# Global queries' pieces of an attention step: from its middle, into a half of the score bank, to its end, into the output bank of the step before

## The chip, the cores and the metric

One core of a Trainium2 chip runs the whole program in one launch. The metric is device time in microseconds; lower is better. TensorE does matrix products and transposes, VectorE (DVE in the rows) and ScalarE (ACT) read PSUM and work element by element, GpSimd (POOL) does some element work in SBUF, SyncE (SP) issues the transfers.

## The reference, cut to what matters

```python
# attention (batch 4, 8 heads, 512 local and 32 global tokens, head size 64, window 32)
s_g = scale * np.matmul(q_g, k_all.transpose(0, 1, 3, 2))
out_g = np.matmul(sm(s_g), v_all)
s_ll = np.where(mask, s_ll, -1000000000.0)      # mask: |i - j| <= 32
s_l = np.concatenate([s_lg, s_ll], axis=-1)
out_l = np.matmul(sm(s_l), np.concatenate([v_g, v_l], axis=2))
# dense layer on 2176 tokens, 512 -> 2048 -> 512
h = x @ w_in
g = np.maximum(h, 0.0) + alpha * np.minimum(h, 0.0)
x = g @ w_out
# 8 experts, 272 tokens each
h = np.maximum(x[mask] @ w1[e], 0.0)
out[mask] = h @ w2[e]
```

## The kernel before, in words

The program has three parts: attention, a dense layer over all tokens, and the experts. The change touches attention alone, the first 148 us.

Attention goes over 16 units (a batch and two heads); two units make a pair `p`, and a pair is done in four **steps** `j` = 0 to 3 of 128 local queries each, so there are 32 steps `n = 4p + j`, and three more in which the pipeline runs empty. The order on TensorE, VectorE and ScalarE is that in which `attention()` calls its helpers (`manual_schedule`); each engine takes its instructions strictly in that order. One turn of the loop holds work of four steps of the pipeline:

- `scores(n)`: TensorE writes the scores into two PSUM banks `s[0]` and `s[1]`, one for each head, 256 of 512 columns each (L387). VectorE makes four masked reductions of them (L393, out `pr` and the row maxima `mx`), ScalarE four exponentials (L395), GpSimd adds a small number to the sums (L397).
- `ptrans(n-1)`: four transposes of the probabilities (L403), copied to SBUF by ScalarE (L405, `pt`).
- `pv(n-2)`: probabilities by values into the lower 256 columns of an output bank `o` (L415); `norm` divides on VectorE (L421, L423).
- `oturn(n-3)`: the normalised output is transposed back into the upper 256 columns of its own `o` bank (L430), and copied into `xb` (L432), by VectorE in odd turns and by ScalarE in even ones.

There are two `o` banks, so the bank that `oturn` reads in turn `n` is the one that `pv` writes in turn `n+1`. Before turn 12 TensorE also makes two products of no use into `o` (L545) in most turns; from turn 12 on `dense.products` puts six products of the dense layer there (L613), with a negative part on ScalarE (L576, `neg`), the activation on VectorE (L591, `g`) and a rounding on ScalarE (L72, `ghi`). `fill` puts in the decoding of weights from float64: L83 and L72 on ScalarE, L85, L88, L90, L92 on VectorE, two or four of them in a turn.

The **global queries** of a pair are done in four pieces, one in a turn, by `wide_part`: in `j` = 1 `gscores` (L449; two reductions L456 on VectorE, then one long exponential L460 on ScalarE), in `j` = 3 `gtrans` (six transposes L472, copies L473 on both engines), in `j` = 0 of the next pair `gpv` (L482, scaled by VectorE, L485), in `j` = 2 `gturn` (L492, copied by VectorE, L493). Before the change they stand after the dense products and ahead of `pv`, and write into the unused upper half of `s[1]` of the same turn (`gscores` and `gtrans` also into a bank of their own, `gs` and `gt`).

Of the kernel before, what the change touches and what calls it, by code (L numbers as in the profile page):

```python
# [25 lines left out]
def tile_attention_moe_moe(ctx: ExitStack, tc: tile.TileContext, qkw, vw,  # L26
# [285 lines left out]
    with ExitStack() as at:  # L312
# [57 lines left out]
        def scores(p, j):  # L370
# [9 lines left out]
            s = d["s"] = [bank([128, 512], "s") for _ in range(2)]  # L380
            for pr in range(2):
                for h, r in heads():
                    for w in range(2):
                        i = 4 * j + 2 * pr + w
                        for a in range(2):
                            u = 2 * p + a
                            T.matmul(s[h][lane(w, a), pr * KW:pr * KW + KW], queries(u, i)[r], U[u]["k"][r, kpos(i):kpos(i) + KW],  # L387
                                     start=True, stop=True)
            for ii in range(4):
                pr, h = divmod(ii, 2)  # L390
                m = mask[:, 0 if j == pr == 0 else 2 if j == STEPS - 1 and pr else 1]
                sc = d["pr", j][:, ii]
                V.tensor_tensor_reduce(out=sc, in0=s[h][:, pr * KW:pr * KW + KW], in1=m, scale=-D ** -0.5, scalar=BIG,  # L393
# [46 lines left out]
        def gscores(p, part):  # L440
            d = G[p]
            if part == 0:
                d["mx"] = gp.tile([128, 4], F32, name="gmx", bufs=2)
            mx = d["mx"]
            s = d["s"][1][:, 256:256 + SG] if part else bank([128, S], "gs0")
            for a in range(2):
                k = U[2 * p + a]["k"]
                x = k[:, WIN:2 * WIN] if part else k[:, GO:GE + WIN].rearrange("p (m c) -> p m c", c=3 * WIN)[:, :, :2 * WIN]
                T.matmul(s[64 * a:64 * a + 64], U[2 * p + a]["g"], x, start=True, stop=True)  # L449
            if part:  # L450
                to, x, z = gsc[:, 2 * WIN:3 * WIN], s, gzero.to_broadcast([128, SG])
            else:
                to = gsc[:, :GE + WIN - GO].rearrange("p (m c) -> p m c", c=3 * WIN)[:, :, :2 * WIN]
                x = s.rearrange("p (m c) -> p m c", c=2 * WIN)
                z = gzero.unsqueeze(2).to_broadcast([128, S // (2 * WIN), 2 * WIN])
            V.tensor_tensor_reduce(out=to, in0=x, in1=z, scale=-D ** -0.5, scalar=mx[:, 0:1] if part else BIG,  # L456
                                   op0=OP.add, op1=OP.min, accum_out=mx[:, part:part + 1])
            if part:
# [3 lines left out]
                later.append(lambda: V.reciprocal(mx[:, 3:4], mx[:, 2:3]))  # L462

        def gtrans(p, part):
            d = G[p]
            n = 2 if part else 4
            t = d["s"][1][:, 256:].rearrange("p (n q) -> p n q", q=128) if part else bank([128, n, 128], "gt0")
            if not part:
                d["t"] = gp.tile([128, len(GW), 128], F32, name="gt")
            for i in range(n):  # L470
                o = kpos(GW[4 * part + i]) - GO
                T.transpose(t[:, i], d["p"][:, o:o + KW], ident)  # L472
            soon.append(lambda: (V.tensor_copy if part else A.copy)(d["t"][:, 4 * part:4 * part + n], t))  # L473

        def gpv(p, s):
            d = G[p]
            o = s[:, 256:256 + D]
# [7 lines left out]
            soon.append(lambda: V.tensor_scalar(d["o"], o, d["mx"][:, 3:4], None, op0=OP.mult))  # L485

        def gturn(p, s):
# [1059 lines left out]
```

## Time and profile before

| | us |
|---|---|
| median of 3 runs | 806.9 (805.6 to 809.14) |
| the profiled execution, its own time | 810.19 |
| its span, first to last instruction | 808.4 |
| TensorE busy | 767.9 (95%) |
| VectorE busy | 439.8 (54%) |
| ScalarE busy | 390.2 (48%) |

In the rows, "PE" is TensorE's products and "PEld" its weight loads; a bracket at the end of a row says how long the engine stood idle before it and what ended that. Ends of matmuls are modelled, so starts are what to read there. Rows of the same instruction that follow each other on VectorE and ScalarE start somewhat before the one ahead has ended, so what an instruction takes of its engine is read from start to start.

### The profile page before, as it was taken

The page shows a single profiled execution, that of the slowest core. Times are in us where ns is not written, and L with a number is a line of the kernel's source. Part 1 is how long each engine was busy: PE and PEld are TensorE (multiplying, and loading weights), DVE is VectorE, ACT ScalarE, POOL GpSimd, SP SyncE. Part 2 cuts the span into 40 slices and gives each one's busy share as a digit, 9 for nine tenths or more (in the row PEclk, how much of TensorE's full clock was granted, in tenths as well). Part 3 has the DMA queues.
Part 4 walks back from the last instruction along what each step waited for, and adds up shares of the span by engine and source line. Part 5 has one row for each costly group of instructions (what it writes and reads, how often), then busy time and mean ns, then how long its engine had stood idle before and what let it go on. Part 6 is the DMA issues. An engine that isn't in the chain of part 4 may idle for free.

```text
span 808.4 us, 21039 instructions
## 1 busy us (share of the span) xinstructions
PE 767.9 (95%) x8386; PEld 710.8 (88%) x8386; DVE 439.8 (54%) x1555; ACT 390.2 (48%) x967; POOL 367.7 (45%) x348
## 2 busy tenths in 40 slices
PE   6788889998999999999999999999899999999996
PEld 4556667998999989999999999999899999989994
DVE  4778887365445621433433467777667777651210
ACT  5768788344544543333332425342455554454430
POOL 2233333144443552100000738573699988688611
PEclk9999999999999999999999999999999999999999
DMA  9978893532343102012211236243376757557510
GB/s 342 385 267 318 287 345 129 202 106 86 118 134 103 63 30 83 29 56 81 88 58 55 84 100 221 92 142 98 106 208 212 207 190 206 155 175 212 192 46 28
DMA packets 53851, 121.98 MB, mean 151 GB/s; under 512 B 4600, under 2 KB 26040, under 8 KB 51705
## 3 DMA queue, kind: packets, MB, share of 16 engines
q1 hardware_dynamic: 50825, 111.73, 42.4%
q0 software_dynamic: 2928, 8.92, 3.1%
q8 instruction: 65, 1.06, 0.5%
q14 instruction: 33, 0.27, 0.1%
HBM read 102.80 MB, written 17.83 MB: 149 GB/s over the span
## 4 chain that ended last, share of the span: by engine, by line
PE 75%; DVE 7%; DMA 5%; issue 5%; ACT 4%; POOL 3%; SPq 0%; POOLq 0%; ACTq 0%; DVEq 0%
PE h L200 21%; PE h L1303 10%; PE h L1147 10%; PE y L239 9%; PE h L1167 8%; DMA raw<-in_moe_w_dram 2%; PE o L415 2%; DMA raw<-in_moe_w_in_dram 2%; PE h L1380 2%; PE t L403 2%; PE lp L282 2%; POOL m L73 2%; PE s L387 2%; DVE pr L393 1%; DMA xpart<-xd 1%
## 5 line engine op out<-in xcount | busy, mean ns | idle before, releaser
L73 POOL TENSOR_TENSOR m<-raw,m 128x1024 fp32r<-128x1024 f32 x64 | 152.2, 2398 | 16.8 <-ACT m L72 15.1
L200 PE MATMUL h<-xh,win 128*128 128x272 f32 x704 | 139.7, 293 | 2.3 <-ACT xd L245 2.3
L200 PEld LDWEIGHTS h<-xh,win 128*128 128x128 f32 x704 | 113.0, 190 | 4.6 <-ACT xd L245 2.5
L73 POOL TENSOR_TENSOR gr<-gb,gr 128x272 fp32r<-128x272 f32 x64 | 48.0, 773 | 148.9 <-ACT gr L72 148.5
L1147 PE MATMUL h<-xsh,m 128*128 128x272 f32 x512 | 103.3, 294 | 0.0
L200 PE MATMUL h<-xl,win 128*128 128x272 f32 x352 | 102.0, 290 | 0.0
L1303 PE MATMUL h<-gr,wout 128*128 128x272 f32 x672 | 95.1, 294 | 0.0
L1167 PE MATMUL h<-hh,m 128*128 128x272 f32 x448 | 91.4, 295 | 0.0
L1303 PEld LDWEIGHTS h<-gr,wout 128*128 128x128 f32 x672 | 87.0, 189 | 0.4 <-ACT gr L72 0.4
L239 PE MATMUL y<-ghi,wout 128*128 128x272 f32 x448 | 86.9, 290 | 0.0
L73 POOL TENSOR_TENSOR glo<-g,ghi 128x272 fp32r<-128x272 f32 x64 | 55.1, 868 | 69.3 <-ACT ghi L72 51.8
L72 ACT CAST m<-raw 128x1024 fp32r<-128x1024 f32 x64 | 66.0, 1050 | 40.1 <-DMA raw<-in_moe_w_dram 39.7
L1147 PEld LDWEIGHTS h<-xsh,m 128*128 128x128 f32 x512 | 81.7, 188 | 0.1
L205 ACT ACTIVATE neg<-h 128x272 f32<-128x272 f32 x120 | 47.6, 397 | 70.3 <-PE h L200 69.0
L1147 PE MATMUL h<-xsl,m 128*128 128x272 f32 x256 | 74.0, 292 | 0.0
L206 DVE SCALAR_TENSOR_TENSOR g<-neg,al,h 128x272 f32<-128x272 f32 x56 | 27.4, 496 | 84.4 <-ACT neg L205 71.5
L1167 PEld LDWEIGHTS h<-hh,m 128*128 128x128 f32 x448 | 71.4, 188 | 0.9 <-issue 0.9
L239 PEld LDWEIGHTS y<-ghi,wout 128*128 128x128 f32 x448 | 70.9, 188 | 0.8 <-issue 0.8
L200 PEld LDWEIGHTS h<-xl,win 128*128 128x128 f32 x352 | 67.1, 191 | 0.0
L1167 PE MATMUL h<-hl,m 128*128 128x272 f32 x224 | 65.8, 294 | 0.0
L239 PE MATMUL y<-glo,wout 128*128 128x272 f32 x224 | 64.5, 288 | 1.1 <-POOL glo L73 1.1
L206 DVE SCALAR_TENSOR_TENSOR gb<-neg,al,h 128x272 f32<-128x272 f32 x64 | 31.3, 496 | 58.8 <-ACT neg L205 58.8
(294 smaller groups left out, 1601.8 us busy)
## 6 DMA issues: line engine op xcount, KB each, us to landing
raw<-in_moe_w_dram SPq DMA_DIRECT2D x64, 512.0 KB, 4.4
vv<-in_v_dram SPq DMA_DIRECT2D x16, 1024.0 KB
qk<-in_qk_dram SPq DMA_DIRECT2D x14, 720.0 KB, 10.1
raw<-in_moe_w_in_dram SPq DMA_DIRECT2D x16, 512.0 KB, 3.9
raw<-in_moe_w_out_dram SPq DMA_DIRECT2D x16, 512.0 KB, 3.6
xb<-xs SPq DMA_DIRECT2D x15, 544.0 KB, 4.0
xs<-xb SPq DMA_DIRECT2D x16, 272.0 KB, 6.4
xpart<-xd SPq DMA_DIRECT2D x32, 136.0 KB, 3.1
```

The costliest lines, as they stand in the source:

```text
L72: a = A.copy(hi, src)
L73: return a, (lo_eng or V).tensor_tensor(lo, src, hi.bitcast(F32), op=OP.subtract)
L200: T.matmul(ps, wi[:, w, k, fs], x[:, k], start=i == 0, stop=i == 3 * KD - 1)
L205: A.activation(out=neg, in_=ps, func=AF.Relu, scale=-1.0)
L206: epi[0] = V.scalar_tensor_tensor(g, neg, al1[:, hf * KH + f:hf * KH + f + 1], ps, op0=OP.mult, op1=OP.add)
L239: T.matmul(ps, wo[:, w, f, ds_], x[:, f], start=f == 0 and i == 0, stop=f == KH - 1 and i == 2)
L282: T.matmul(lp[r:r + 32], w, x, start=n < 4, stop=n >= LT - 4)
L387: T.matmul(s[h][lane(w, a), pr * KW:pr * KW + KW], queries(u, i)[r], U[u]["k"][r, kpos(i):kpos(i) + KW], start=True, stop=True)
L403: T.transpose(t[:, ii], d["pr", j][:, ii], ident)
L1147: T.matmul(ps, d["w1"][:, w, kk, f * 128:(f + 1) * 128], x[:, kk], start=kk == 0 and i == 0, stop=kk == KD - 1 and i == 2)
L1167: T.matmul(ps, d["w2"][:, w, f, ms], x[:, f], start=i == 0, stop=i == 3 * K3 - 1)
L1303: T.matmul(ps[j], wo[:, w, f, ds_], x, start=f == 0 and a == 0, stop=f == KH - 1 and a == 2)
```

## The change: what it does, and the diff

`wide_part` is called after `oturn`, at the end of a turn, and its instructions write into `prev`, the `o` bank of the turn before, columns 0 on, whose lower half `norm` has read by then. The copy into `xb` is taken out of `oturn` into `oput` and stands behind the pieces. The readers of the pieces on VectorE and ScalarE move with them: behind `norm` and behind the copy `pt`. The score banks hold 256 columns only. `gscores` goes unit by unit, and its reciprocal moves to `gtrans`.

```diff
-            s = d["s"] = [bank([128, 512], "s") for _ in range(2)]
+            s = [bank([128, 2, KW], "s") for _ in range(2)]
...
+        def oput(p, j):
+            d = G[p]
+            o = d["o", j]
             x = d["x"][:, :, SG + QS * j:SG + QS * j + QS].rearrange("p a (w q) -> p w a q", q=WIN)
             at_out[0] = (A.copy if j % 2 else V.tensor_copy)(x, o[:, 256:].rearrange("p (w a q) -> p w a q", a=2, q=WIN))
 
...
-        def gscores(p, part):
...
+        def gscores(p, free):
             d = G[p]
-            if part == 0:
-                d["mx"] = gp.tile([128, 4], F32, name="gmx", bufs=2)
-            mx = d["mx"]
-            s = d["s"][1][:, 256:256 + SG] if part else bank([128, S], "gs0")
+            d["mx"] = mx = gp.tile([128, 4], F32, name="gmx", bufs=2)
+            s = (bank([128, S], "gs0"), free[:, :SG])
             for a in range(2):
...
+            def rest_():
+                V.tensor_tensor_reduce(out=gsc[:, :GE + WIN - GO].rearrange("p (m c) -> p m c", c=3 * WIN)[:, :, :2 * WIN],
+                                       in0=s[0].rearrange("p (m c) -> p m c", c=2 * WIN),
+                                       in1=gzero.unsqueeze(2).to_broadcast([128, S // (2 * WIN), 2 * WIN]),
+                                       scale=-D ** -0.5, scalar=BIG, op0=OP.add, op1=OP.min, accum_out=mx[:, 0:1])
+                V.tensor_tensor_reduce(out=gsc[:, 2 * WIN:3 * WIN], in0=s[1], in1=gzero.to_broadcast([128, SG]), scale=-D ** -0.5,
+                                       scalar=mx[:, 0:1], op0=OP.add, op1=OP.min, accum_out=mx[:, 1:2])
                 d["p"] = gp.tile([128, GE - GO], F32, name="gpr")
                 A.activation(out=d["p"], in_=gsc[:, :GE - GO], func=AF.Exp, bias=mx[:, 1:2], scale=-1.0, accum_out=mx[:, 2:3])
                 P.tensor_scalar(mx[:, 2:3], mx[:, 2:3], 1e-9, None, op0=OP.add)
-                later.append(lambda: V.reciprocal(mx[:, 3:4], mx[:, 2:3]))
...
+        def gtrans(p, free):
             d = G[p]
-            n = 2 if part else 4
-            t = d["s"][1][:, 256:].rearrange("p (n q) -> p n q", q=128) if part else bank([128, n, 128], "gt0")
-            if not part:
-                d["t"] = gp.tile([128, len(GW), 128], F32, name="gt")
-            for i in range(n):
-                o = kpos(GW[4 * part + i]) - GO
-                T.transpose(t[:, i], d["p"][:, o:o + KW], ident)
-            soon.append(lambda: (V.tensor_copy if part else A.copy)(d["t"][:, 4 * part:4 * part + n], t))
-
-        def gpv(p, s):
...
-        later, soon, at_out = [], [], [None]
-
-        def wide_part(n):
+        at_out = [None]
+
+        def wide_part(n, free):
             p, j = divmod(n, STEPS)
-            last = n - STEPS * NU // 2
-            if last >= 0:
-                s = bank([128, 512], "s") if last in (0, 1) else None
-            else:
-                s = G[p]["s"][1]
-            if j == 1 and last < 0:
-                gscores(p, 0)
-                gscores(p, 1)
+            last = n >= STEPS * NU // 2
+            if j == 0 and p:
+                gpv(p - 1, free)
+            if j == 1 and not last:
+                gscores(p, free)
+            if p and (j == 2 or last and j == 1):
+                gturn(p - 1, free)
             if j == 3:
-                gtrans(p, 0)
-                gtrans(p, 1)
-            if p and j == 0:
-                gpv(p - 1, s)
-            if p and (j == 2 or last == 1):
-                gturn(p - 1, s)
+                gtrans(p, free)
 
...
                 dense.products(n)
-                if n < N + 2:
-                    wide_part(n)
-                while soon:
-                    soon.pop(0)()
                 fill("V", 2 if n >= SOLO and n % 3 == 0 else 1 if n < SOLO else 0)
...
                     ptrans(*divmod(n - 1, STEPS))
                 if n >= 3:
                     oturn(*divmod(n - 3, STEPS))
+                if n < N + 2:
+                    wide_part(n, bank([128, 512], "o") if n == 1 else prev)
+                if n >= 3:
+                    oput(*divmod(n - 3, STEPS))
+                prev = o
                 if p and j == 3:
                     gout(p - 1)
```

What this does to the order. In turn 13 (`j` = 1) on TensorE stood, before (`s` the score banks, `gs` a bank of its own, `o` the output bank, `t` transposed probabilities):

```order
L449 MATMUL gs_1200<-qk 64x512 x2
L449 MATMUL s<-qk 64x32 [waits DVE_49]
L449 MATMUL s<-qk 64x32
L415 MATMUL o<-vv,pt 32x64 [waits Activation_49]
L415 MATMUL o<-vv,pt 32x64 x15
L403 MATMUL t<-ident,pr 128x128 x4
L430 MATMUL o<-ident,on 128x128 x2
L387 MATMUL s<-qk 32x128 [waits PE_49]
```

and there stands now, in the same turn, with the head of the next turn's scores and the `pv` of that turn behind it:

```order
L414 MATMUL o<-vv,pt 32x64 [waits Activation_49]
L414 MATMUL o<-vv,pt 32x64 x15
L402 MATMUL t<-ident,pr 128x128 x4
L429 MATMUL o<-ident,on 128x128 x2
L450 MATMUL gs_1229<-qk 64x512
L450 MATMUL o<-qk 64x32
L450 MATMUL gs_1229<-qk 64x512
L450 MATMUL o<-qk 64x32
L387 MATMUL s<-qk 32x128 [waits DVE_49,PE_49]
...
L414 MATMUL o<-vv,pt 32x64 [waits DVE_49,DMAHW0_49,PE_49,Activation_49]
```

The global pieces have gone behind the transposes and lost their wait for VectorE; the wait for VectorE stands at the next turn's `pv`.

On ScalarE, from the end of turn 13 over turn 14 (`j` = 2), stood before:

```order
L460 ACTIVATE gpr,gmx<-gsc,gmx 128x736 [waits DVE_49]
L405 COPY pt<-t 128x512 [waits PE_49]
L576 ACTIVATE neg<-h_1087 128x272
L395 ACTIVATE pr,sm<-pr,mx 128x128 [waits DVE_49,Activation_49]
L395 ACTIVATE pr,sm<-pr,mx 128x128 [waits DVE_49] x3
L72 CAST ghi<-g 128x272 [waits DVE_49]
L405 COPY pt<-t 128x512 [waits PE_49,Activation_49]
L432 COPY xb<-o 128x4x2x32 [waits PE_49]
```

and there stands now:

```order
L404 COPY pt<-t 128x512 [waits PE_49]
L460 ACTIVATE gpr,gmx<-gsc,gmx 128x736 [waits DVE_49]
L568 ACTIVATE neg<-h_1088 128x272
L394 ACTIVATE pr,sm<-pr,mx 128x128 [waits DVE_49,Activation_49]
L394 ACTIVATE pr,sm<-pr,mx 128x128 [waits DVE_49] x3
L72 CAST ghi<-g 128x272 [waits DVE_49]
L404 COPY pt<-t 128x512 [waits PE_49,Activation_49]
L435 COPY xb<-o 128x4x2x32 [waits DVE_49]
```

The long exponential of the global queries has changed places with the copy `pt`, and the copy into `xb` waits for VectorE where it waited for TensorE.

On VectorE, in turn 13, stood before:

```order
L456 ISA gsc,gmx<-gs_1200,gzero 128x8x64 [waits PE_49]
L456 ISA gmx 128x1
L456 ISA gsc,gmx<-s,gzero,gmx 128x32 [waits DVE_49,PE_49]
L456 ISA gmx 128x1
L421 RECIPROCAL sm<-sm 128x4
L423 TENSOR_TENSOR on<-o,sm 128x256 [waits DVE_49,PE_49]
L432 COPY xb<-o 128x4x2x32 [waits PE_49]
```

and there stands now:

```order
L420 RECIPROCAL sm<-sm 128x4
L422 TENSOR_TENSOR on<-o,sm 128x256 [waits DVE_49,PE_49]
L453 ISA gsc,gmx<-gs_1229,gzero 128x8x64 [waits PE_49]
L453 ISA gmx 128x1
L457 ISA gsc,gmx<-o,gzero,gmx 128x32 [waits DVE_49,PE_49]
L457 ISA gmx 128x1
L435 COPY xb<-o 128x4x2x32
```

The reductions of the global scores have gone behind the normalisation, and the copy into `xb` stands behind them.

## Rows read from the trace of the kernel before

**Rows 1.** Busy time by stretch: length, PE, PEld, DVE, ACT, POOL, granted clock, DMA share, GB/s.
```profile
200.00:260.00 60.00, 60.00 (x480) 59.01 (x479) 30.74 (x50) 29.13 (x64) 25.84 (x25) 1.00 0.39 120
```

**Rows 2.** The same view of a stretch of attention.
```profile
100.00:120.00 20.00, 17.85 (x429) 13.52 (x424) 17.97 (x79) 17.62 (x60) 7.50 (x11) 1.00 0.90 326
```

**Rows 3.** Waits, 0 to 150 us: who, for whom; total us, times, longest.
```profile
PE s L482 <- ACT pr L395: 3.1, 3, 1.6
...
PE s L492 <- DVE mx L393: 1.9, 5, 0.9
...
PE s L482 <- DVE mx L393: 1.6, 4, 0.6
...
PE s L472 <- DVE mx L393: 1.0, 2, 0.7
```

**Rows 4.** Timeline, TensorE, turns 13, 21, 25, 29: start, us, instruction.
```profile
60.53 0.67 PE L387 MATMUL s<-qk 64*32 64x128 f32 x32
...
95.76 0.67 PE L387 MATMUL s<-qk 64*32 64x128 f32 x32
97.30 1.08 PE L449 MATMUL gs<-qk 128*64 128x512 f32 x4
...
99.82 0.32 PE L415 MATMUL o<-vv,pt 128*32 128x64 f32 x7 [0.84 <-issue]
...
112.84 0.67 PE L387 MATMUL s<-qk 64*32 64x128 f32 x32
...
130.70 0.67 PE L387 MATMUL s<-qk 64*32 64x128 f32 x32
```

**Rows 5.** Timeline, turn 16 (`j` = 0), VectorE and TensorE.
```profile
75.77 0.08 DVE L393 DVE_READ_ACCUMULATOR2_ANT mx<- 128x1 f32 x1
...
76.00 1.01 PE L482 MATMUL s<-vv,gt 128*32 128x64 f32 x48 [1.56 <-ACT pr L395]
...
78.33 0.67 PE L387 MATMUL s<-qk 64*32 64x128 f32 x32
```

**Rows 6.** Timeline, VectorE and ScalarE, end of turn 13 and turn 14.
```profile
63.95 0.68 DVE L456 CUSTOM_DVE_ANT_1 gsc<-gs,gzero 128x512 f32<-128x512 f32 x1
...
65.08 0.91 ACT L460 ACTIVATE gpr<-gsc,gmx 128x736 f32<-128x736 f32 x1 [1.13 <-DVE gmx L456]
...
65.73 0.42 DVE L432 COPY xb<-o 128x256 f32<-128x256 f32 x1
...
66.33 0.29 DVE L393 CUSTOM_DVE_ANT_0 pr<-s,mask 128x128 f32<-128x128 f32 x1 [0.18 <-PE s L387]
...
66.45 0.40 ACT L576 ACTIVATE neg<-h 128x272 f32<-128x272 f32 x1
...
66.74 0.40 ACT L395 ACTIVATE pr<-pr,mx 128x128 f32<-128x128 f32 x1
...
67.26 0.48 DVE L591 SCALAR_TENSOR_TENSOR g<-neg,al,h 128x272 f32<-128x272 f32 x1
...
67.65 0.68 DVE L90 SCALAR_TENSOR_TENSOR mag<-raw,mag 128x512 int32<-128x512 int32 x1
...
68.28 0.41 ACT L72 CAST ghi<-g 128x272 fp32r<-128x272 f32 x1
...
68.92 0.59 ACT L405 COPY pt<-t 128x512 f32<-128x512 f32 x1 [0.22 <-PE t L403]
...
68.98 0.22 DVE L493 COPY xb<-s 128x64 f32<-128x64 f32 x1
...
69.39 0.42 DVE L423 TENSOR_TENSOR on<-o,sm 128x256 f32<-128x256 f32 x1
...
69.40 0.38 ACT L432 COPY xb<-o 128x256 f32<-128x256 f32 x1
```

**Rows 7.** Timeline, the longest stand of TensorE in attention.
```profile
44.22 0.42 PE L387 MATMUL s<-qk 64*32 64x128 f32 x7 [2.59 <-issue]
```

**Rows 8.** Busy time by stretch, behind that stand; the granted clock is third from the end.
```profile
44.00:48.00 4.00, 3.78 (x53) 2.63 (x53) 3.02 (x14) 1.47 (x7) 0.45 (x1) 0.68 0.14 18
```

More of the change, by code (lines that the diff above doesn't have):

```diff
@@ L386, in scores @@
                             u = 2 * p + a
[L387 removed]
+                            T.matmul(s[h][lane(w, a), pr], queries(u, i)[r], U[u]["k"][r, kpos(i):kpos(i) + KW],
                                      start=True, stop=True)
             for ii in range(4):
[L390 to L391 removed]
+                m = mask[:, 0 if j == 0 and ii < 2 else 2 if j == STEPS - 1 and ii >= 2 else 1]
                 sc = d["pr", j][:, ii]
[L393 removed]
+                V.tensor_tensor_reduce(out=sc, in0=s[ii % 2][:, ii // 2], in1=m, scale=-D ** -0.5, scalar=BIG,
                                        op0=OP.add, op1=OP.min, accum_out=d["mx", j][:, ii:ii + 1])
@@ L438, in glane @@
             return slice(SG * (2 * a + h), SG * (2 * a + h + 1))
-        def gscores(p, part):
+        def gscores(p, free):
             d = G[p]
-            if part == 0:
-                d["mx"] = gp.tile([128, 4], F32, name="gmx", bufs=2)
-            mx = d["mx"]
-            s = d["s"][1][:, 256:256 + SG] if part else bank([128, S], "gs0")
+            d["mx"] = mx = gp.tile([128, 4], F32, name="gmx", bufs=2)
+            s = (bank([128, S], "gs0"), free[:, :SG])
             for a in range(2):
                 k = U[2 * p + a]["k"]
[L448 to L451, printed above, removed]
-            else:
[L453 to L458, printed above, removed]
+                for part, x in enumerate((k[:, GO:GE + WIN].rearrange("p (m c) -> p m c", c=3 * WIN)[:, :, :2 * WIN], k[:, WIN:2 * WIN])):
+                    T.matmul(s[part][64 * a:64 * a + 64], U[2 * p + a]["g"], x, start=True, stop=True)
+            def rest_():
[5 more added lines that the diff above has]
+                                       scalar=mx[:, 0:1], op0=OP.add, op1=OP.min, accum_out=mx[:, 1:2])
                 d["p"] = gp.tile([128, GE - GO], F32, name="gpr")
@@ L461, in gscores, with gpv @@
                 P.tensor_scalar(mx[:, 2:3], mx[:, 2:3], 1e-9, None, op0=OP.add)
-                later.append(lambda: V.reciprocal(mx[:, 3:4], mx[:, 2:3]))
-        def gtrans(p, part):
+            rest_()
+        def gtrans(p, free):
             d = G[p]
-            n = 2 if part else 4
-            t = d["s"][1][:, 256:].rearrange("p (n q) -> p n q", q=128) if part else bank([128, n, 128], "gt0")
-            if not part:
-                d["t"] = gp.tile([128, len(GW), 128], F32, name="gt")
-            for i in range(n):
-                o = kpos(GW[4 * part + i]) - GO
-                T.transpose(t[:, i], d["p"][:, o:o + KW], ident)
-            soon.append(lambda: (V.tensor_copy if part else A.copy)(d["t"][:, 4 * part:4 * part + n], t))
-        def gpv(p, s):
+            V.reciprocal(d["mx"][:, 3:4], d["mx"][:, 2:3])
+            d["t"] = gp.tile([128, len(GW), 128], F32, name="gt")
+            t = (bank([128, 4, 128], "gt0"), free[:, :256].rearrange("p (n q) -> p n q", q=128))
+            for i, w in enumerate(GW):
+                o = kpos(w) - GO
+                T.transpose(t[i // 4][:, i % 4], d["p"][:, o:o + KW], ident)
+            A.copy(d["t"][:, :4], t[0])
+            V.tensor_copy(d["t"][:, 4:], t[1])
+        def gpv(p, free):
             d = G[p]
-            o = s[:, 256:256 + D]
+            o = free[:, :D]
             for n, w in enumerate(GW):
@@ L492, in gturn @@
                 T.matmul(o[r], d["o"], i[:, h], start=True, stop=True)
[L493 removed]
+            V.tensor_copy(d["x"][:, :, :SG], o.rearrange("p (a q) -> p a q", q=SG))
         def gout(p):
@@ L536, in attention @@
                     scores(p, j)
-                while later:
-                    later.pop(0)()
                 dense.close(n)
@@ L564, in attention @@
                 yield 0
-            while later:
-                later.pop(0)()
             gout(NU // 2 - 1)
```

9 lines of the change are left out of this document (4 added, 5 removed).

## The prediction

> **What bounds the kernel now.** I read the busy time by stretch first. Behind attention TensorE is busy the whole stretch [rows 1], so a time won or lost in attention is passed on to the end nearly whole; the change touches nothing there. In attention no engine is full, and three come close: VectorE 18.0, ScalarE 17.6, TensorE 17.9 of 20 us [rows 2]. So this part is bound by how the three wait for each other. The table of waits says where TensorE stood for VectorE at the global pieces: 3.1 + 1.9 + 1.6 + 1.0 = 7.6 us in all of attention [rows 3]. The timeline shows what that wait is: in turn 16 VectorE ends its reductions of the local scores at 75.85, and `gpv` starts at 76.00 [rows 5]. It has nothing to do with these reductions, it only writes into another half of the bank that they read. The row names ScalarE as releaser, but its start follows VectorE's end by 0.15.
>
> Four turns, a period, take (130.70 - 60.53) / 4 = 17.5 us [rows 4]; one of them, turns 21 to 24, 112.84 - 95.76 = 17.1. In it TensorE stands 0.84 us for nothing that the profile shows, in `pv` of `j` = 1; such a stand comes once a period, and I keep it.
>
> **What is removed.** The four waits of rows 3: the pieces now write into a bank whose readers ended a turn ago. That is 7.6 us of TensorE over 8 periods, 0.95 a period. Products, transposes and passes are the same in number and size, so this is all there is to gain, and only if nothing else becomes late.
>
> **What is added, first part: the long exponential comes late.** Before, `gscores` stands early in the turn; VectorE reduces at 63.95, ScalarE begins the exponential at 65.08, and is back for `neg` of the next turn at 66.45, 0.12 behind the start of that turn's reductions at 66.33. VectorE gets its `neg` in time, and does L591 at 67.26 [rows 6]. Now the same products are the last of the turn. VectorE can't start before they end, ScalarE not before VectorE is through, and behind the exponential stand two decode passes, and only then `neg`. VectorE's L591 waits for that, and the decode passes, `norm` and the readers of the global pieces are queued behind L591.
>
> **Second part: the copy into `xb` in even turns.** ScalarE does it, and before it waited for TensorE alone. Turn 14: VectorE's reader of the global piece at 68.98, its `norm` at 69.39, ScalarE's copy at 69.40 [rows 6]. Now the bank of that copy also holds the global piece, the copy waits for VectorE's reader of it, and that stands behind `norm`. Who waits for the copy: the next turn's `pv`, which writes into this bank, and on ScalarE two decode passes and the next four exponentials. Before, `pv` waited for the copy too, but TensorE's check on VectorE was the end of the current turn's reductions; now it is the end of all of the turn before. The two lie just one set of reductions, 0.9 us, apart, so the new order gives VectorE only that much more room.
>
> The Trainium skill, in "PSUM — Partial Sum Buffer", section "PSUM bank collisions raise a hardware error", says that two engines must not touch one bank in the same partitions at a time, different columns or not, and that waits have to be set by the bank. Rows 5 agree (disjoint columns, and the wait is there), and by this rule the second part can't be taken out while piece and copy share a bank. Were it not for it, the sum below would be about +2 in place of +4.9.
>
> **The sum.** I lay out turns 21 to 24 in the new order: each instruction starts when the one ahead on its engine and what it waits for are done. What each takes is read from start to start. TensorE: 1.54 from a turn's scores to the next piece (95.76 to 97.30), 1.1 for `gscores` [rows 4], 0.6 `pv`, 0.5 and 0.3 the transposes. VectorE: reductions 0.9, L591 0.4, decode passes 0.5 to 0.7, `norm` with its reciprocal 0.6, global reductions 1.0 (63.95 to 65.08 less the hand-over), copy into `xb` 0.4. ScalarE: `neg` 0.3, exponentials 1.5 (66.74 to 68.28), `pt` 0.5, `xb` 0.3, the long one 0.9, two decode passes 1.2 [rows 6]. With the scores of turn 21 at 0:
> - Turn 21: TensorE's `pv` at 2.3 (with the stand of 0.84), transposes from 3.0, `gscores` 3.8 to 4.9. VectorE: reductions 0.7 to 1.6, four decode passes 2.2 to 4.7, `norm` to 5.3, global reductions to 6.3, `xb` to 6.7. ScalarE: exponentials to 3.6, `pt` to 4.2, idle, the long one 6.5 to 7.4, decode to 8.6.
> - Turn 22, scores at 4.9: `pv` could start at 6.5 and waits for `xb` until 6.9; the turn ends at 8.7. VectorE ends its reductions at 7.5 and **stands 1.5 us** for `neg`; L591 at 9.0, two decode passes, `norm`, the copy of `gturn` at 10.9. ScalarE: exponentials 8.8 to 10.4, `ghi`, `pt` to 11.3, `xb` to 11.7.
> - Turn 23, scores at 8.7: `pv` could start at 10.2 and **waits for `xb` until 11.8**; the turn ends at 14.0.
> - Turn 24, scores at 14.0: `pv` at 15.5 without a wait, the turn ends at 18.0.
>
> So 18.0 against 17.1 in the trace. The same lay-out in the old order gives 17.3 for these turns, and 71.0 for turns 13 to 28, where the trace has 70.2: it is good to about 1%. In the new order turns 13 to 28 come to 73.8, which is 0.7 a period more. The four periods differ, by how many decode passes fall on `j` = 2: from +0.2 to +0.9. Where four fall there, `pv` of the next turn waits some 3 us. Periods ahead of turn 12 have the useless products ahead of `pv`, which write into the bank as well and so wait 0.9 earlier; I take 0.7 there too. The first period waits for its transfers. Seven periods at 0.7 are **+4.9 us**, with ends 7 x 0.2 = +1.4 and 7 x 0.9 = +6.3. One more switch of shape on TensorE in `j` = 0 lies beside these waits and costs nothing.
>
> The profiled execution took 810.19, 3.3 above the median; the difference is put on the median: 806.9 + 4.9 = 811.8. Half a per cent, about what a measurement of this kernel can tell from no change, is 4.0 us: 802.9 to 810.9 counts as the same.
>
> **The rivals.**
> - *Slower, as above*: 811.8. For it: the waits that the order now shows on VectorE at `pv` and at the `xb` copy. Chance 0.54; in it a tenth or so for all periods like the worst (four decode passes on `j` = 2 of the laid-out kind, +1.5 each), 817 or more.
> - *Even*: the new waits eat what the old ones give, and no more. The point that decides is when `neg` in `j` = 2 starts: were ScalarE there when VectorE ends its reductions (7.5, not 8.6 in the lay-out), the 1.5 us of VectorE and the 1.6 us of TensorE behind it would fall away, and a period would be under the old 17.3. If ScalarE's passes are some tenths shorter than I took them, half of this goes, 0.7 a period becomes 0, and the time is 807. Against it: the exponential can't start before 4.9 + 1.0 + hand-overs. Chance 0.36.
> - *Faster*: TensorE's four waits go and little comes back. All of it would be 806.9 - 7.6 = 799.3, half of it 803.1; I put 802 on it. For it: in the laid-out period TensorE's own work is 18.0 - 0.4 - 1.6 = 16.0, 1.5 under the 17.5 of now. Against it: VectorE's 18.0 of 20 leaves room for a tenth at most, and now its work comes at the end of the turn, when TensorE needs it most. Chance 0.10.
> - Beside these, a scatter that hits any case: at 44.22 TensorE had stood 2.59 us [rows 7], and behind that the granted clock was 0.68 on average [rows 8], between its two levels of 1.2 and 2.4 GHz. In the new order such a stand may be shorter, longer or elsewhere: 2 us either way.
>
> **How the numbers follow.** The even case spans 802.9 to 810.9, the slower one from 810.9 up. With 0.1 left out at each end, and the scatter of the runs (805.6 to 809.14) and of the stand taken in, the range is 804 to 816.5. Faster 0.10, same 0.36, slower 0.54.
>
> **What would show it right or wrong.** Right: the waits of rows 3 are gone; TensorE's starts of `pv` (o banks) wait in `j` = 3 and `j` = 2 for the `xb` copy or VectorE, over 1 us a period; the long exponential starts about 6.5 after its turn's scores, `neg` in `j` = 2 some 3.7 behind its turn's scores, and L591 waits for it; ScalarE's `xb` copy waits for VectorE; the period is about 18.2. Wrong: a period under 17.5 with TensorE waiting for nothing at `pv`; or attention unchanged and the difference behind 148 us.

## The result: slower by 5 us, and the profile after

The changed kernel took 813.8 us in the median (811.5 to 817.14), the kernel before 808.6 beside it: a ratio of 1.0073, 95% interval 1.0050 to 1.0096. A second measurement gave 811.8 against 808.2, ratio 1.0051 (1.0023 to 1.0078). So it is slower, by 5.2 us in the first measurement and by 3.6 in the second. The forecast was 811.8 us, with slower as the likeliest case.

The profiled execution took 817.14 with a span of 815.4, 7.0 more than the span before; that is more than the medians differ, and the clock has a share in it (below). The page's first part, busy time and share:

```profile
PE 772.3 (95%) x8386; PEld 714.0 (88%) x8386; DVE 439.8 (54%) x1555; ACT 388.4 (48%) x967; POOL 368.2 (45%) x348
```

The work is the same: VectorE and ScalarE are busy as long as before. TensorE's 4 us more are slower products, not more of them: the count of 8386 is that of the page before. Busy time by stretch, columns as in [rows 1], of the changed kernel:

```profile
100.00:120.00 20.00, 17.16 (x420) 13.00 (x405) 16.89 (x73) 15.98 (x54) 7.83 (x12) 1.00 0.87 290
...
200.00:260.00 60.00, 60.00 (x479) 59.84 (x479) 35.35 (x56) 29.93 (x69) 28.30 (x28) 1.00 0.38 117
```

Behind attention TensorE is as full as in [rows 1]: a loss in attention reaches the end. In attention all three engines have become emptier than in [rows 2]: from 100 to 120 us VectorE 16.9 in place of 18.0, ScalarE 16.0 in place of 17.6. They wait more for each other. The scores of turn 31 start at 146.27, before at 138.20, and from there to the end it is 1.1 us less than before: the whole loss lies in attention. (In a second pair of profiled executions, below, turn 31 starts at 141.76 and 139.62.)

The table of waits of the changed kernel, 0 to 155 us (who, line, for whom; total, times, longest):

```profile
ACT gpr L460 <- DVE gmx L457: 15.5, 8, 3.1
...
ACT xb L435 <- DVE go L485: 8.4, 8, 1.8
...
DVE gsc L453 <- PE o L450: 7.9, 6, 2.7
...
PE o L538 <- ACT xb L435: 3.4, 2, 1.9
...
ACT xb L435 <- DVE xb L493: 2.9, 4, 1.2
...
DVE g L583 <- ACT neg L568: 2.9, 4, 1.3
...
PE o L538 <- DVE xb L435: 2.7, 4, 1.0
...
PE o L414 <- ACT neg L568: 1.8, 1, 1.8
```

The same table of the kernel before, for the two rows of VectorE and the one of the long exponential:

```profile
ACT gpr L460 <- DVE gmx L456: 8.9, 8, 1.5
...
DVE gsc L456 <- PE gs L449: 1.0, 1, 1.0
...
DVE g L591 <- ACT neg L576: 0.2, 1, 0.2
```

The waits of [rows 3] are gone. In their place TensorE waits for the bank of `pv`, at L414 or, before turn 12, at the useless products of L538 ahead of it. Two waits are new on VectorE: 7.9 us for the products of `gscores` (`gsc`, before 1.0) and 2.9 for `neg` (before 0.2). The first was not in my forecast. Whether these two waits are what costs the time is the question of the experiments.

The timeline shows one such turn, 13 into 14, where [rows 6] shows it before (start, us, instruction, in brackets the idle time ahead and its releaser):

```profile
65.07 0.26 PE L450 MATMUL o<-qk 128*64 128x32 f32 x4
65.27 0.67 PE L387 MATMUL s<-qk 64*32 64x128 f32 x32
...
65.87 0.68 DVE L453 CUSTOM_DVE_ANT_1 gsc<-gs,gzero 128x512 f32<-128x512 f32 x1
...
67.00 0.91 ACT L460 ACTIVATE gpr<-gsc,gmx 128x736 f32<-128x736 f32 x1 [1.18 <-DVE gmx L457]
...
67.22 0.28 DVE L392 CUSTOM_DVE_ANT_0 pr<-s,mask 128x128 f32<-128x128 f32 x1
...
67.91 0.38 ACT L568 ACTIVATE neg<-h 128x272 f32<-128x272 f32 x1
...
68.32 0.50 DVE L583 SCALAR_TENSOR_TENSOR g<-neg,al,h 128x272 f32<-128x272 f32 x1 [0.18 <-ACT neg L568]
```

`gscores` are now the last products of the turn; behind them come VectorE's global reductions, the long exponential, and only then `neg`, 0.7 us behind the start of that turn's reductions, where it was 0.12 [rows 6]. And the reductions themselves start 1.95 us after their scores (67.22 less 65.27), since the global ones stand ahead of them.

### The profile page after: what moved, and what is told of

Read it like the earlier page. It is cut to its first block, busy times and chain, and to the rows that moved or that the text cites. A ratio compares the mean times of both kernels' runs of the same rounds, so it can differ in the third digit from the quotient of the medians.

```text
span 815.4 us, 21090 instructions
## 1 busy us (share of the span) xinstructions
PE 772.3 (95%) x8386; PEld 714.0 (88%) x8386; DVE 439.8 (54%) x1555; ACT 388.4 (48%) x967; POOL 368.2 (45%) x348
## 3 DMA queue, kind: packets, MB, share of 16 engines
q8 instruction: 66, 1.08, 0.5%
## 4 chain that ended last, share of the span: by engine, by line
PE 70%; DVE 8%; DMA 7%; issue 5%; ACT 4%; POOL 4%; SPq 0%; POOLq 0%; DVEq 0%; ACTq 0%
PE h L200 21%; PE h L1295 10%; PE y L239 9%; PE h L1159 7%; PE h L1139 7%; DMA raw<-in_moe_w_dram 3%; POOL m L73 2%; DMA raw<-in_moe_w_in_dram 2%; PE t L402 2%; PE o L414 2%; PE h L1372 2%; PE lp L282 2%; PE gs L450 1%; DMA xpart<-xd 1%; PE pc L975 1%
## 5 line engine op out<-in xcount | busy, mean ns | idle before, releaser
L1159 PEld LDWEIGHTS h<-hh,m 128*128 128x128 f32 x448 | 71.4, 188 | 0.9 <-issue 0.9
```

The source lines that it names most:

```text
L1159: T.matmul(ps, d["w2"][:, w, f, ms], x[:, f], start=i == 0, stop=i == 3 * K3 - 1)
```

## The experiments

Each edit is against the changed kernel, if nothing else is said. Beside them the kernel before stood at 808.0 to 808.3 us.

### Which half of the change: order or bank

The order alone: the pieces at the end of the turn, but into the half of the score bank that they used before.

```
-            s = [bank([128, 2, KW], "s") for _ in range(2)]
+            s = d["s"] = [bank([128, 512], "s") for _ in range(2)]
...
-                    wide_part(n, bank([128, 512], "o") if n == 1 else prev)
+                    wide_part(n, (d_s(n) if n < N else bank([128, 512], "s"))[:, 256:])
```

`d_s(n)` is the second score bank of turn `n`.

> The pieces stand at the end of the turn as in the changed kernel, but write into the upper half of this turn's score bank s[1], as before. So the order is moved and the bank is not: the xb copy on ScalarE waits for TensorE alone again, and the next turn's scores of the second head wait for VectorE's reader of the piece. If the bank shared with the xb copy were the cause (theory B), this would be near the kernel before, 807 to 810. If the place at the end of the turn is the cause, with its late exponential and late readers (theory A), it is as slow as the changed kernel or slower: the scores then wait at the head of the turn for a reader that stands behind norm, 815 to 825.

Measured: 816.5, ratio 1.0098 (1.0066 to 1.013). TensorE's waits at the scores, in that kernel:

```profile
PE s L387 <- DVE xb L493: 5.3, 5, 2.4
PE s L387 <- DVE gmx L457: 5.2, 6, 1.0
PE s L387 <- DVE gt L473: 2.4, 5, 1.0
```

With 1.7 us more for `go` that is 14.6 us: now the next scores, not `pv`, wait for VectorE's readers. This kernel has waits of its own, so it doesn't give the price of the order, but it shows that the order doesn't pay without the other bank.

The bank alone: the pieces in the middle of the turn, as before the change, into the preceding step's output bank.

```
                 dense.products(n)
+                if n < N + 2:
+                    wide_part(n, bank([128, 512], "o") if n == 1 else prev)
                 fill("V", 2 if n >= SOLO and n % 3 == 0 else 1 if n < SOLO else 0)
...
                     oturn(*divmod(n - 3, STEPS))
-                if n < N + 2:
-                    wide_part(n, bank([128, 512], "o") if n == 1 else prev)
```

> The pieces stand in the middle of the turn, ahead of pv, as in the kernel before, but write into the output bank of the turn before, as in the changed kernel. So the bank is moved and the order is not. TensorE need not wait for the reductions of the same turn; the xb copy waits for VectorE's reader, which stands ahead of norm. Theory A (order): the loss is gone and some of the old waits with it, 804 to 808, about 2 us under the kernel before. Theory B (bank): still slow, 811 to 815.

Measured: 805.7, ratio 0.9971 (0.9951 to 0.9991): 2.3 us under the kernel before. The small edits that came with the bank (the reciprocal moved to `gtrans`, `gscores` unit by unit) are in it too, so none of these is the loss: the loss is the order. The gain is small beside the 7.6 us of [rows 3], and the waits say why:

```profile
PE o L429 <- DVE xb L493: 5.2, 6, 1.1
PE o L429 <- DVE gmx L457: 2.3, 3, 0.9
...
PE o L429 <- DVE gt L473: 0.7, 1, 0.7
PE o L429 <- DVE go L485: 0.6, 2, 0.3
```

The pieces no longer wait, but the transposes `oturn` behind them write into the same bank and wait for the pieces' readers, 8.8 us. The columns are not the same. The Trainium skill asks for this in "PSUM — Partial Sum Buffer", section "PSUM bank collisions raise a hardware error": semaphores are to guard PSUM by the bank (strictly, by the bank and a quarter of its partitions), not by the address. The trace agrees: the wait is there though the columns differ. The wait stands later in the turn, behind `pv` and `ptrans`; I take that to be why it costs less, but no run shows it apart.

### The two parts that I had named

The long exponential put off into the next turn, behind `neg` and the local exponentials:

```
+            def exp_():
                 A.activation(out=d["p"], in_=gsc[:, :GE - GO], func=AF.Exp, bias=mx[:, 1:2], scale=-1.0, accum_out=mx[:, 2:3])
                 P.tensor_scalar(mx[:, 2:3], mx[:, 2:3], 1e-9, None, op0=OP.add)
             rest_()
+            later.append(exp_)
...
                     scores(p, j)
+                while later:
+                    later.pop(0)()
                 dense.close(n)
```

> The changed kernel, with the long exponential of the global queries put into the next turn, behind neg and the four local exponentials; it is needed two turns later only. Theory A: neg starts in time, VectorE doesn't wait for it, and some 3 to 4 us of the 5 come back: 809 to 811. If the exponential's place is not the cause (B, or the end of the turn as such), it stays at 813 to 815.

Measured: 811.8, ratio 1.0048 (1.0026 to 1.0069). The expectation of 809 to 811 was missed. Against the first measurement of the changed kernel (813.8) 2 us come back, against the second (811.8) nothing, so a gain isn't shown, though VectorE's wait for `neg` is gone from the table. The other wait stayed:

```profile
DVE gsc L453 <- PE o L450: 8.4, 7, 2.3
```

The second part: the readers of `gpv` and `gturn` on ScalarE in even turns, so that its `xb` copy waits for nobody.

```
-            V.tensor_scalar(d["o"], o, d["mx"][:, 3:4], None, op0=OP.mult)
+            A.activation(out=d["o"], in_=o, func=AF.Copy, scale=d["mx"][:, 3:4])
...
-            V.tensor_copy(d["x"][:, :, :SG], o.rearrange("p (a q) -> p a q", q=SG))
+            (V.tensor_copy if last else A.copy)(d["x"][:, :, :SG], o.rearrange("p (a q) -> p a q", q=SG))
```

> The changed kernel, with the readers of the pieces in even turns (the scaling of gpv, the copy of gturn) on ScalarE in place of VectorE, so that the xb copy behind them waits for no other engine; VectorE has 0.33 us a period less to do, ScalarE 0.5 more. Theory B: ScalarE's wait for VectorE of 11.3 us in all goes, and 3 to 5 us come back: 809 to 811. Theory A: VectorE is late anyway, and what is behind is late with it: 812 to 815.

Measured: 812.2, ratio 1.0069 (1.0042 to 1.0096), not to be told from the changed kernel. Both edits together:

> The changed kernel with both single repairs at once: the long exponential put off behind the next turn's `neg` and local exponentials, and the readers of `gpv` and `gturn` in even turns put on ScalarE, which then waits for nobody when it copies from the same bank. Alone they stood at 811.8 and 812.2 us, against 813.8 for the changed kernel and 808.0 for the kernel before. If the two parts of my theory are two causes of the loss, they add up: 813.8 - 2.0 - 1.6 = 810.2, so 809 to 811, and about 2 us of the loss stay, which would be the order itself (VectorE's work comes at the end of the turn). If they are one and the same slack seen twice, the time is that of the better one, 811.5 to 812.5. If the loss were all in these two, the time would be 808 or less.

Measured: 811.4, ratio 1.0034 (1.0014 to 1.0055). That is no better than the first alone, within the intervals: the two parts as I had named them are at most some 2 of the 5 us.

The late exponential in the kernel with the bank alone, where the pieces stand in the middle (both edits above):

> The pieces stay in the middle of the turn, as before the change, but write into the output bank of the preceding turn (805.7 us alone), and the long exponential is put off behind the next turn's `neg` and local exponentials. If a late exponential is bad only in the new order, where it stands between VectorE's last reduction and `neg`, it gives nothing here: 805 to 807. If it also frees ScalarE for `neg` in the middle order, 803 to 805, which would be the fastest of all. If it now makes `gtrans` wait, two turns later, over 807.

Measured: 807.4, ratio 0.9989 (0.9976 to 1.0003), no better than the bank alone at 805.7, and just over the 807 of the third case. `gtrans` itself has no wait in the trace, but `oturn` waits 2.0 us for its reader (0.7 with the bank alone). So in the middle order putting the exponential off gains nothing.

### Is it VectorE's backlog

VectorE's two extra decode passes moved from every third turn to the turns with `j` = 0:

```
-                fill("V", 2 if n >= SOLO and n % 3 == 0 else 1 if n < SOLO else 0)
+                fill("V", 2 if n >= SOLO and n % 4 == 0 else 1 if n < SOLO else 0)
```

> The changed kernel with VectorE's two extra decode passes, which stand in every third turn, put in the turns with j = 0 instead (seven turns in place of nine, so four passes are left for later). My theory says that `pv` waits for VectorE's end of the turn before, most of all where the extra passes fall on j = 2 or 3 next to the piece's reader and the copies. With the passes always in j = 0, where VectorE's piece is the short `gpv` reader, the loss falls by much of its size: 808 to 811. If it is not VectorE's backlog but the fixed chain piece, reader, copy, `pv` that sets the time, it stays at 812.5 to 815.

Measured: 815.7, ratio 1.0097 (1.0061 to 1.0133). The expectation of 808 to 811 was wrong, and the time is above the other case too. But the time alone says little: in the profiled execution turn 31 starts at 139.96 (138.20 and 139.62 in the kernel before, 146.27 and 141.76 in the changed one), and from there to the end it takes 673.1 us, where the four executions of these two kernels take 667.4 to 670.2. The four passes that it leaves for later are the likely price. The waits:

```profile
DVE gsc L453 <- PE o L450: 9.6, 6, 2.4
...
DVE g L583 <- ACT neg L568: 0.7, 4, 0.2
```

VectorE is early here: it hardly waits for `neg`, and all the more for `gscores`. And TensorE waits for VectorE and ScalarE only 1.5 us in turns 13 to 28, where it waits 5.6 and 6.2 in the two executions of the changed kernel. So in this execution the backlog was behind those waits, as I had thought. What came in their place the table below shows.

### Which piece

So I split the pieces. First `gscores` alone back to the middle, the other three at the end:

```
                 dense.products(n)
+                if n < N + 2 and j == 1:
+                    wide_part(n, bank([128, 512], "o") if n == 1 else prev)
...
-                if n < N + 2:
+                if n < N + 2 and not (j == 1):
                     wide_part(n, bank([128, 512], "o") if n == 1 else prev)
```

> The changed kernel with one of the four pieces, `gscores` in j = 1, moved back to the middle of the turn; the other three stay at its end, and all write into the preceding step's bank. All four in the middle stood at 805.7 us, all four at the end at 813.8. If the loss comes from the one piece that two engines must work through before the next `neg` (VectorE's global reductions, then the long exponential), this gets nearly all of it back: 806 to 808.5. If each piece at the end costs its share, a quarter to a half comes back: 810 to 812.5.

Then the complement, with `j != 1` in both conditions: `gscores` alone at the end.

> The complement: `gscores` alone stands at the end of its turn, `gturn`, `gtrans` and `gpv` in the middle, all into the preceding step's bank. If `gscores` at the end is the loss, the time stays near the changed kernel's: 810.5 to 813.5. If each piece costs its share, 806.5 to 809.

Measured: 808.3, ratio 0.9995 (0.9974 to 1.0016), with `gscores` in the middle; 812.9, ratio 1.0063 (1.0038 to 1.0088), with `gscores` alone at the end. Both are as expected, and together they show it: one piece of four, `gscores`, carries the loss. The waits of the first, `gscores` in the middle:

```profile
ACT gpr L460 <- DVE gmx L457: 8.9, 8, 1.4
ACT xb L435 <- DVE go L485: 8.8, 8, 2.7
...
DVE gsc L453 <- PE o L450: 1.2, 1, 1.2
...
DVE g L585 <- ACT neg L570: 0.2, 1, 0.2
```

and of the second, `gscores` at the end:

```profile
ACT gpr L460 <- DVE gmx L457: 13.2, 8, 1.9
...
DVE gsc L453 <- PE o L450: 5.8, 6, 2.2
...
DVE g L585 <- ACT neg L570: 3.0, 5, 1.3
```

The three waits go with the piece: 8.9, 1.0 and 0.2 before, nearly the same with `gscores` in the middle, up with `gscores` at the end. ScalarE's wait for the readers (`xb` for `go`) is 8.8 us in the kernel that loses nothing against before: that one costs little. From the kernel with the bank alone (805.7) `gscores` at the end costs 4.7 + 2.3 = 7.0 us, the other three at the end 0.1 + 2.3 = 2.4; the last is at the edge of what the intervals can tell.

How the piece's place reaches TensorE is less plain. TensorE's idle time in attention is of two kinds: waits for VectorE or ScalarE, and stands for which the profile names no releaser ("issue" in the brackets; "stands" in the table). Summed over turns 13 to 28 (the idle times that the timeline shows in brackets), in us:

| kernel (two executions of "before" and "changed", one of the others) | waits | stands | together | median |
|---|---|---|---|---|
| before | 4.9, 6.1 | 3.6, 2.4 | 8.5, 8.5 | 808.0 to 808.6 |
| bank alone | 5.5 | 0.5 | 6.0 | 805.7 |
| bank alone, late exponential | 6.5 | 0.6 | 7.1 | 807.4 |
| `gscores` in the middle | 5.7 | 3.3 | 9.0 | 808.3 |
| `gscores` alone at the end | 7.5 | 3.9 | 11.4 | 812.9 |
| changed | 5.6, 6.2 | 5.8, 6.3 | 11.4, 12.5 | 813.8, 811.8 |
| late exponential | 7.2 | 4.0 | 11.2 | 811.8 |
| readers on ScalarE | 3.1 | 8.0 | 11.1 | 812.2 |
| both edits | 2.9 | 7.8 | 10.7 | 811.4 |
| passes in `j` = 0 | 1.5 | 9.5 | 11.0 | 815.7 |
| order alone | 11.7 | 0.0 | 11.7 | 816.5 |

Together they are 10.7 to 12.5 us in every kernel with `gscores` at the end and 6.0 to 9.0 in every other one, but how they divide changes from kernel to kernel. Where an edit took waits away (readers on ScalarE, passes in `j` = 0), the stands were longer by most of it, and the medians fell little or not at all. So a wait that is gone from the table is not yet time won.

### The clock

In the first profiled execution TensorE's clock fell after the longer idle times. Turn 16, TensorE and VectorE:

```profile
76.30 0.42 DVE L435 COPY xb<-o 128x256 f32<-128x256 f32 x1
...
76.86 0.89 PE L414 MATMUL o<-vv,pt 128*32 128x64 f32 x32 [1.84 <-ACT neg L568]
77.68 1.12 PE L402 MATMUL t<-ident,pr 128*128 128x128 f32 x4
...
83.20 0.66 PE L402 MATMUL t<-ident,pr 128*128 128x128 f32 x4
```

`pv` stood 1.84 us; the row names ScalarE, but VectorE's copy from its bank ends 0.14 ahead of it. Behind it four transposes take 1.12 in place of 0.66. The granted clock was 0.57 from 77 to 81 us, 0.50 in its middle, the lower of the two levels:

```profile
77.00:81.00 4.00, 4.00 (x102) 3.06 (x104) 2.35 (x12) 2.42 (x10) 1.37 (x3) 0.57 0.90 347
```

To see what that is worth, eleven useless products kept TensorE busy ahead of two such waits, in turns 11 and 16:

```
+        def busy(t):
+            for _ in range(11):
+                T.matmul(t[:, 0], ident, ident, start=True, stop=True)
...
+                t = bank([128, 4, 128], "t") if 1 <= n <= N else None
+                if n == 11:
+                    busy(t)
...
                 dense.products(n)
+                if n == 16:
+                    busy(t)
```

> The changed kernel with eleven useless products of 128x128 (some 0.16 us each, 1.7 us in all) on TensorE, in turn 11 ahead of the useless products that are there already, and in turn 16 ahead of `pv`: the two places where the profiled execution of the changed kernel stood 1.59 and 1.84 us for the `xb` copies and where the granted clock then was at 0.50 for some 4 us. They write into the bank of the transposes, which is free by then, so nothing waits for them. If it is the standing that brings the clock down, the two stretches of half clock near 54 and 77 us are gone from the trace, the mean clock rises, and the time is 1 to 3.5 us under the changed kernel's 813.8, with more products than it has. If the clock falls for another reason, the stretches stay, and the time is 813.8 to 816.

Measured: 817.1, ratio 1.0102 (1.0035 to 1.0169), above both cases, with wide scatter. In the profiled execution of this kernel:

```profile
72.26 2.62 PE L520 MATMUL t<-ident 128*128 128x128 f32 x22
74.81 0.65 PE L413 MATMUL o<-vv,pt 128*32 128x64 f32 x32
```
```profile
76.00:80.00 4.00, 3.26 (x93) 2.30 (x95) 1.83 (x12) 1.69 (x6) 0.92 (x2) 1.00 0.53 205
89.00:93.00 4.00, 2.96 (x41) 2.79 (x42) 3.15 (x14) 3.39 (x12) 1.94 (x3) 0.58 1.01 345
```

`pv` has no wait and the full clock behind it, as meant. But the products took 2.62 us, not the 1.7 that I had put on them, and other stretches at half clock stand at 89, 117 and 134 us. A gain is not shown, and the price of the clock can't be had from this run. Nor is it shown that the products kept the clock up: in the second execution of the changed kernel, which has no such products, `pv` of turn 16 stands the same 1.84 us and the full clock follows:

```profile
74.27 0.65 PE L414 MATMUL o<-vv,pt 128*32 128x64 f32 x32 [1.84 <-DVE xb L435]
```
```profile
75.00:79.00 4.00, 3.56 (x103) 2.70 (x103) 3.54 (x16) 3.48 (x16) 0.99 (x2) 1.00 0.78 307
```

That second execution is one of two more that say how much of the clock is the execution's. The changed kernel and the kernel before, again:

> The changed kernel again, for a second profiled execution. Its first one stood 7.2 us without a releaser on TensorE between 18 and 150 us and lost 8.5 us of granted clock. If these belong to the program, the stands come at the same places in the instruction stream and the clock falls behind the same waits; if they are the execution's, at others. The median: 812.5 to 815.

> The kernel before again, for a second profiled execution: its first one had the long stand at 44 us, 8.3 us of stands without a releaser, and lost 1.7 us of granted clock in attention. If these belong to the program, the same places and some 8 and 2 us again; if they are the execution's, other ones. The time: 806 to 811.

Measured: 811.8 for the changed kernel, somewhat under the 812.5 to 815 expected; one run of 810.4 for the kernel before. The profiled spans are 809.2 and 808.1, only 1.1 apart, where the first two were 7.0 apart. Their mean clocks go with that: 0.987 and 0.995 in the first two, 0.994 and 0.989 in the second. Over all runs the mean clock of the changed kernel is 0.992, of the kernel before 0.994; by the difference of 0.0018 that is some 1.5 us of 808. And at a like clock the loss is still there: of the runs with a mean clock of 0.995 or more, five of the changed kernel have a median of 812.4, eighteen of the kernel before 807.7. So most of the 5 us is idle time at any clock. The waits are much alike. In the second execution of the changed kernel:

```profile
DVE gsc L453 <- PE o L450: 5.5, 5, 2.2
...
DVE g L583 <- ACT neg L568: 2.9, 4, 1.3
```

## Why the prediction was right, step by step

- **What bounds the kernel** held: the loss stays in attention and arrives at the end, and with the waits of VectorE and ScalarE up, all three engines are emptier.
- **What is removed** held: the four waits of [rows 3] are gone, 7.6 us. That nothing more than this could be won held too: even with the pieces in the middle, 2.3 us remain of it.
- **TensorE's new wait at `pv`** held in sum, but not as the place of the loss. L414 and L538 wait for `xb` and VectorE 12.8 us in the table of the changed kernel: 3.4 + 2.7 + 1.8, and 1.9, 1.6 and 1.4 in rows of the same table that aren't shown. Less the 7.6, and less 1.5 of such waits before, that is a net 3.7 us; the forecast had 4.9 by the sum of seven periods. In the second execution it is 13.8 in place of 12.8. But the waits rose in turns 4 to 12, from 3.5 and 3.0 us in the two executions before to 6.3 and 6.6, while the stands there fell from 4.7 and 3.7 to 1.4 and 0.9, and these nine turns took no longer: 41.7 and 39.7 us, before 41.6 and 41.4. In turns 13 to 28, where the time was lost, the waits hardly changed (table above).
- **First part, the late exponential.** In the turns that were laid out it came nearly as forecast. Turn 21 starts at 99.53, turn 22 at 104.92:

```profile
106.17 0.91 ACT L460 ACTIVATE gpr<-gsc,gmx 128x736 f32<-128x736 f32 x1 [1.82 <-DVE gmx L457]
...
108.16 0.39 ACT L568 ACTIVATE neg<-h 128x272 f32<-128x272 f32 x1
...
108.58 0.50 DVE L583 SCALAR_TENSOR_TENSOR g<-neg,al,h 128x272 f32<-128x272 f32 x1 [1.27 <-ACT neg L568]
```

The exponential starts 6.6 after its turn's scores, `neg` 3.2 after its own (4.0 in the second execution), and VectorE stands 1.27; the forecast had 6.5, 3.7 and 1.5. But in turns 13 and 25 no decode pass stands between the exponential and `neg`; there `neg` starts 2.6 and 2.2 after its turn's scores and VectorE stands 0.18. So the chain was given too much in the sum, 2.9 us of VectorE's time in all, and taken out it gives back 2 us at most.
- **What was missing** is the term that the forecast kept: TensorE's stands, "0.84 us, once a period". In turns 13 to 28 they grew from 3.6 and 2.4 us to 5.8 and 6.3, and the clock lost 5.1 and 1.7 us where it had lost none and 1.7. Turn 23 shows the exchange: `pv` was to wait 1.6 us for the `xb` copy; it waited for nothing, and TensorE stood 1.17 us in the scores ahead of it. The turn took 5.2 us against 5.3 by the lay-out, by another cause. In the same way `pv` of turn 19, behind four decode passes on `j` = 2, was to wait some 3 us; it waited 0 and 0.5, behind a stand of 1.60.
- **VectorE's stand for the products of `gscores`** was not in the forecast either. In the laid-out turn VectorE found them ready, as forecast; in the others it waits, 7.9 and 5.5 us in all. It is not shown to cost anything: with the passes in `j` = 0 it is longest, 9.6 us, and TensorE's waits are the shortest of all, 1.5.
- **Second part, the `xb` copy**, held as a wait (8.4 + 2.9 us) and not as a price: 8.8 us of it stand in the kernel that equals the one before. With it falls the sentence that without the shared bank the sum would be about +2: with the wait taken off ScalarE the kernel stood at 812.2.
- **The period** was 18.2 by forecast. In the first execution turns 13 to 28 took 138.77 - 61.02 = 77.8 us, 19.4 a period, three stretches at half clock among them; in the second 134.26 - 58.60 = 75.7, 18.9, with one. The kernel before took 70.2 and 71.4, 17.5 and 17.9. The laid-out turns 21 to 24 took 17.9 and 17.5, before 17.1 both times, near the 18.0 forecast; the other periods lost more. So these four periods lost 1.1 to 1.9 each, where the forecast had 0.7, and the three ahead of them nothing: turn 13 starts at 61.02 and 58.60, before at 60.53 and 60.69, where the forecast had +2.1.
- **The sum** of +4.9 agrees with +5.2 and +3.6 by luck in part. The direction, and the order as its cause, were right. But the early periods were given 2.1 us that they didn't lose, the four late ones 2.8 where they lost 7.6 and 4.2; `neg` and the `xb` copy were given too much, the stands without a releaser and the clock no more than a scatter.
- **The rivals.** Faster would have needed the order to cost nothing; 805.7 is what the change gives without it. Even is what it gives with `gscores` left in the middle.

What stays open: how `gscores` at the end makes TensorE's idle time longer. That it does is shown both ways, by the kernel with it alone at the end and the one with it alone in the middle. But no edit of the chain behind it (the exponential, the readers, VectorE's passes) took the time back, and why the waits that these edits removed returned as stands no run shows. The sums of idle time are of one or two executions of each kernel.

## What to carry to other kernels

A piece of work that two engines hand on before a third can go on (products, VectorE's reduction, ScalarE's long exponential) belongs early in a step, with independent work behind it; moved to the end, its whole chain lies between this step and the next, even if every wait that it had is gone. Here that cost 7.0 us. A change that moves several pieces at once is best tried piece by piece: here three moved at little cost, and the fourth brought most of the loss. And the bank move alone was the better change, 805.7 us. To judge an edit by the trace, add up all idle time of the engine that bounds the kernel, with or without a releaser: a wait that goes may come back as a stand.

## What I had not expected of the hardware

TensorE's stands without a releaser lie at fixed places of the program; whether one comes there, and how long it is, is the execution's. The first and the second execution of the changed kernel, in that order:

```profile
90.60 0.63 PE L387 MATMUL s<-qk 64*32 64x128 f32 x22 [1.60 <-issue]
...
110.17 0.44 PE L387 MATMUL s<-qk 64*32 64x128 f32 x13 [1.17 <-issue]
...
121.56 0.30 PE L414 MATMUL o<-vv,pt 128*32 128x64 f32 x4 [1.47 <-issue]
```
```profile
88.14 0.63 PE L387 MATMUL s<-qk 64*32 64x128 f32 x22 [1.60 <-issue]
...
107.45 0.44 PE L387 MATMUL s<-qk 64*32 64x128 f32 x13 [0.62 <-issue]
118.60 0.31 PE L414 MATMUL o<-vv,pt 128*32 128x64 f32 x4 [1.00 <-issue]
```

Each falls into the same group of products, with the same number of them left (22, 13, 4), and lasts 1.60, 1.17 and 1.47 or 1.60, 0.62 and 1.00 us. The stand of [rows 7] came again in the second execution of the kernel before, at the same seven last products, with 2.87 us. Counted in the trace, the stands of the kernel before fall on TensorE's products 734, 1116, 1498, 1880 and 2262, 382 apart, with two more at 351 and 606; those of the changed kernel fall on 731, 1613, 1867, 1992, 2245 and 2370, the last five 125 or some 254 apart. Not each place has its stand each time: 1867 has one of 1.06 us in the first execution and 0.25 in the second, 1488 none in the first and 1.72 in the second.

What ends them is in the packed trace, though the brackets don't name it: the page lists a queue "q8 instruction" (66 packets, 1.08 MB, so 16 KB each). In the fourteen profiled executions 73 such stands of over 0.3 us lie between 18 and 150 us, and every one ends 1.2 to 1.6 us after a packet of this queue has ended; from such a packet to the end of a wait for VectorE or ScalarE it is anything from 0 to 8.5 us. I read this as TensorE standing for its own next instructions. The trace doesn't say for which engine a packet is, so that last step is argued.

My forecast of 2 us either way for such a stand's scatter was of the right size for one execution against another (7.2 us of stands in both executions of the changed kernel between 18 and 150 us, 8.3 and 6.1 before); that the change itself would shift them between its turns I had not forecast.

And an idle time of 1.4 to 1.9 us is paid twice when half the clock follows: after the 1.84 us of turn 16 some 4 us ran at 0.57. Not each is followed by it: at 136.44 `pv` had stood 1.62 us, and from 135 to 140 the clock was 1.00; and the same 1.84 us in turn 16 of the second execution had 1.00 behind it.
